# A planned TensorE order that counts the change between 64-row and 128-row matmuls and places like matmuls side by side, with 107 instead of 108 tiles on VectorE

## The chip, the cores and the metric

The kernel runs on one core of one Trainium2 chip. The metric is the device time of one execution in microseconds (us); lower is better. Times are medians of several executions. All the runs used here are undisturbed ("fast"). "Span" is the length of the one execution that was profiled; it is about 2 us shorter than the time that is measured around it.

## The reference, cut to what matters

```python
B, H, S, D = 1, 32, 2048, 640          # head size Dh = D // H = 20

def reference(q, k, v, t):
    eps = 1e-6
    qn = q / (jnp.sqrt((q * q).sum(axis=-1, keepdims=True)) + eps)
    kn = k / (jnp.sqrt((k * k).sum(axis=-1, keepdims=True)) + eps)
    logits = jnp.einsum('bhqd,bhkd->bhqk', qn, kn) * t[None, :, None, None]
    attn = _softmax(logits, axis=-1)
    return jnp.einsum('bhqk,bhkd->bhqd', attn, v)
```

It is attention with normalised q and k, for 32 heads of 2048 rows of 20 numbers. The expensive part is the exponential of 32 x 2048 x 2048 scores. The scores are cut into 512 row-tiles (16 per head), each 128 keys by 2048 queries.

## The kernel before

ScalarE computes the exponential of 404 of the 512 tiles, in 539 "waves" of up to three pieces of 128x512. VectorE computes the other 108 with integer and fp16 arithmetic. TensorE computes all scores (matmuls into `psA` for ScalarE, into `psD` for VectorE) and all sums with the values (matmuls into `psO`).

The three engines run fixed instruction lists. A small planner makes them when the kernel is built: each task has an engine, a duration, dependencies and a priority (lower goes first). The planner steps through time on a clock of its own, and whenever an engine is free it takes the ready task of the lowest priority. What the chip then does is bound to this order, but not to the planner's clock.

```python
    def schedule(self):
        ...                                            # cut
            for e in touched:
                if free[e] > now + 1e-9 or not ready[e]:
                    continue
                _, _, t = heapq.heappop(ready[e])      # lowest priority value
                t.start = now
                t.end = now + t.dur
                if e == "PE":
                    kind = t.name[:2]                  # "qk" or "pv"
                    if kind != last_pe[0]:
                        t.end += 0.09                  # a change of kind
                    last_pe[0] = kind
```

One wave's scores are two tasks. Heads have only 20 rows, zero-padded to 32, so the operands of two pieces from different halves of the array are multiplied at the same time with 64 rows each (the "pair"); the third piece is multiplied with 128 rows. Both tasks are named `qkA`:

```python
    pair = [] if plain else next(([i, i + 1] for i in range(len(us) - 1)
                if A_units[us[i]][2] // 2 != A_units[us[i + 1]][2] // 2), [])
    ...                                                # cut
    qks = [add("PE", f"qkA{w}", lambda e, tk, part=part: f_qk(e, part, 32 if plain else 64 if part is pair else 128),
               PE_MM * (1 if plain or part is pair else len(part)), deps, due_a(us[0]) - 100) for part in parts]
```

VectorE's scores are single 128-row matmuls, one for each 512 columns. They share one PSUM bank, so the next one can only be written when VectorE has read the last (`t1_prev`). Four such reads make a tile, and four more VectorE operations finish it:

```python
    for g in reversed(range(NG)):
        dep = [trn[h]] + rot[h] + (qz0 if h == 0 and j else []) + [t1_prev[0]]
        qk = add("PE", f"qkD{j}.{g}", lambda e, tk, h=h, r=r, g=g, j=j: qk_mm(
            e, h, r, g, psD[:, :], 128 if j else 32), PE_MM, dep, due - 50)
        ...                                            # cut: psD -> xt on VectorE
```

The sums with the values are groups of four matmuls that use 32 columns of the array each (`pvA`, `pve`, `pvs`, `pvt`, priority `due`).

## Time and profile before

| | before |
|---|---|
| time | 755.69 us (755.17 to 755.82, 3 executions); 755.43 us when timed beside the changed kernel |
| span of the profiled execution | 753.2 us |
| exponentials | 539, the shortest time from start to start 1.330 us |
| first exponential starts, last one starts | 14.05 us, 747.58 us |

The page of the profile of the kernel before: the span, the busy time of each engine with its share of the span and its number of instructions, and the shares of the chain of waits that ended last.

```profile
span 753.2 us, 12434 instructions
...
PE 702.4 (93%) x4960; PEld 194.6 (26%) x4960; DVE 719.6 (96%) x1209; ACT 731.7 (97%) x541; POOL 9.2 (1%) x24
...
ACT 59%; PE 23%; DVE 15%; DMA 1%; issue 1%; SPq 0%; DVEq 0%
```

Three engines are over 93% busy. The chain alternates among all of them: 59% ScalarE, 23% TensorE, 15% VectorE. So for 41% of the span it was not ScalarE itself that set the time.

The costliest groups (operation, shapes, count | busy us, mean ns of one | idle us before them and what ended it):

```profile
L489 ACT ACTIVATE p_ring<-psA 128x1536 bf16<-128x1536 f32 x539 | 730.2, 1523 | 15.7 <-PE psA L415 14.5
...
L522 DVE TENSOR_SCALAR xt<-psD 128x512 int16<-128x512 f32 x432 | 295.4, 684 | 23.1 <-PE psD L415 18.6
```

The mean of 1,523 ns is not the pace of ScalarE, because successive exponentials overlap in the record. Their start times are the better measure, and from them I made the following account. Each span splits exactly into four parts: the start of the first exponential; the number of intervals times the floor of 1.330 us; the loss, which is the sum of what each interval has above 1.330 us; and the tail from the start of the last exponential to the end. For before: 14.05 + 538 x 1.330 + 18.00 + 5.64 = 753.2 us. Of the loss, 3.34 us fall before 40 us, in the start, and 14.66 us after.

From the list of waits (engine, line, what it waited for: us in total, times, longest; "PEld" is TensorE's weight load, which comes first and so waits first):

```profile
PEld psA L415 <- ACT p_ring L489: 124.4, 356, 1.0
...
PEld psD L415 <- DVE xt L522: 63.1, 177, 1.3
DVE xt L522 <- PE psD L415: 18.6, 41, 1.2
...
ACT p_ring L489 <- PE psA L415: 14.5, 9, 11.4
```

The last line holds the 11.4 us at the start and little else: most of the misses are too small to show as idle time between overlapping records. The second line is TensorE waiting for VectorE to free the one PSUM bank.

TensorE's timeline near the end of before (start, duration, operation, rows*columns of the array, count):

```profile
739.17 0.40 PE L424 MATMUL psO<-p_ring,vaug 128*32 128x512 bf16 x4
739.50 0.39 PE L415 MATMUL psD<-qz,qkT 128*128 128x512 bf16 x1
739.82 0.39 PE L415 MATMUL psA<-qz,qkT 64*128 64x512 bf16 x2
740.14 0.39 PE L415 MATMUL psA<-qz,kR 128*128 128x512 bf16 x1
740.46 0.40 PE L424 MATMUL psO<-p_ring,vaug 128*32 128x512 bf16 x4
```

Every step changes the shape (32-column values, 128-row score, 64-row pair, 128-row score, values), and from start to start each takes 0.32 or 0.33 us. Over the whole trace, the step from a 128-row score in `psA` to one in `psD` takes 0.227 us in the median, and the step from a 64-row pair to the 128-row score 0.319 us. A change costs some 0.093 us.

### The profile page before, as it was taken

What the parts mean: (1) busy time and instruction counts of PE and PEld (TensorE: products, weight loads), DVE (VectorE), ACT (ScalarE), POOL (GpSimd) and SP (SyncE); (2) the same over time, 40 slices, a digit from 0 to 9 for tenths busy, and PEclk for the clock granted to TensorE, in tenths of its full rate; (3) what the DMA queues carried; (4) which work ended last, traced back from release to release, by engine and by line L of the source; (5) the groups of instructions that cost most, each with busy time, mean ns of one, the idle gap of its engine ahead of it and who ended that gap; (6) DMA issues with size and microseconds to landing.
All of it is one profiled execution on the core that took longest, in us unless ns stands there. A gap on an engine that the chain in (4) does not pass through costs nothing.

```text
span 753.2 us, 12434 instructions
## 1 busy us (share of the span) xinstructions
PE 702.4 (93%) x4960; PEld 194.6 (26%) x4960; DVE 719.6 (96%) x1209; ACT 731.7 (97%) x541; POOL 9.2 (1%) x24
## 2 busy tenths in 40 slices
PE   1999999999999999999999999999999999999997
PEld 0222222222222222222222222222222222222222
DVE  7799999999999999999999999999999999999997
ACT  3899999999999999999999999999999999999997
POOL 4000000000000000000000000000000000000000
PEclk9999999999999999999999999999999999999999
DMA  5533242323423242250323413234141332413000
GB/s 76 84 38 54 42 75 33 73 22 68 53 37 72 24 81 29 55 66 19 78 24 66 55 29 71 21 66 54 37 76 9 82 39 46 70 28 72 5 5 5
DMA packets 197929, 36.49 MB, mean 48 GB/s; under 512 B 173680, under 2 KB 197872, under 8 KB 197872
## 3 DMA queue, kind: packets, MB, share of 16 engines
q1 hardware_dynamic: 197728, 35.62, 29.6%
q8 instruction: 39, 0.64, 0.4%
q14 instruction: 18, 0.15, 0.1%
q10 hardware_dynamic: 144, 0.08, 0.1%
HBM read 7.87 MB, written 2.62 MB: 14 GB/s over the span
## 4 chain that ended last, share of the span: by engine, by line
ACT 59%; PE 23%; DVE 15%; DMA 1%; issue 1%; SPq 0%; DVEq 0%
ACT p_ring L489 59%; PE psA L415 11%; PE psO L424 8%; DVE xt L522 6%; PE psD L415 5%; DVE tt L536 4%; DVE mm L534 1%; DVE ee L530 1%; DVE ss L532 1%; DVE sq L320 1%; DVE rs_sum L322 1%; DMA kR<-kx 1%; SPq L234 0%; DVE qkn L348 0%; DMA qk_sb<-in_k_dram 0%
## 5 line engine op out<-in xcount | busy, mean ns | idle before, releaser
L489 ACT ACTIVATE p_ring<-psA 128x1536 bf16<-128x1536 f32 x539 | 730.2, 1523 | 15.7 <-PE psA L415 14.5
L415 PE MATMUL psA<-qz,kR 64*128 64x512 bf16 (+1 forms) x1209 | 319.0, 389 | 13.9 <-ACT p_ring L489 10.7
L522 DVE TENSOR_SCALAR xt<-psD 128x512 int16<-128x512 f32 x432 | 295.4, 684 | 23.1 <-PE psD L415 18.6
L424 PE MATMUL psO<-p_ring,vaug 128*32 128x512 bf16 x1616 | 152.1, 388 | 0.6 <-DVE oT L436 0.4
L415 PEld LDWEIGHTS psA<-qz,kR 64*128 64x128 bf16 (+1 forms) x1209 | 83.4, 94 | 225.3 <-issue 128.4
L415 PE MATMUL psA<-qz,qkT 64*128 64x512 bf16 (+1 forms) x392 | 128.6, 388 | 4.0 <-ACT p_ring L489 3.2
L536 DVE TENSOR_TENSOR tt<-xt,mm 128x2048 f16<-128x2048 f16 x108 | 131.0, 1213 | 0.2
L415 PE MATMUL psD<-qz,kR 128*128 128x512 bf16 x321 | 124.0, 386 | 6.0 <-DVE xt L522 3.8
L530 DVE TENSOR_SCALAR ee<-xt 128x2048 int16<-128x2048 int16 x108 | 73.7, 682 | 0.4
L534 DVE TENSOR_SCALAR mm<-xt 128x2048 int16<-128x2048 int16 x108 | 73.8, 684 | 0.0
L532 DVE TENSOR_SCALAR ss<-xt 128x2048 int16<-128x2048 int16 x108 | 73.7, 683 | 0.0
L424 PEld LDWEIGHTS psO<-p_ring,vaug 128*32 128x32 bf16 x1616 | 38.5, 94 | 84.6 <-issue 74.9
L415 PEld LDWEIGHTS psA<-qz,qkT 64*128 64x128 bf16 (+1 forms) x392 | 31.3, 94 | 68.9 <-issue 41.5
L415 PEld LDWEIGHTS psD<-qz,kR 128*128 128x128 bf16 x321 | 31.0, 97 | 65.8 <-DVE xt L522 43.6
L424 PE MATMUL psO<-tt,vaug 128*32 128x512 f16 x432 | 42.8, 386 | 3.4 <-DVE tt L536 2.0
L424 PE MATMUL psO<-ee,vaug 128*32 128x512 f16 x432 | 43.1, 389 | 1.5 <-DVE ee L530 1.3
L415 PE MATMUL psD<-qz,qkT 128*128 128x512 bf16 x107 | 41.5, 388 | 2.2 <-DVE xt L522 1.1
L424 PE MATMUL psO<-ss,vaug 128*32 128x512 f16 x432 | 42.7, 386 | 0.1
L320 DVE TENSOR_TENSOR sq<-qk_sb 128x640 f32<-128x640 bf16 x32 | 26.0, 813 | 0.9 <-DMA qk_sb<-in_q_dram 0.9
L322 DVE TENSOR_REDUCE rs_sum<-sq 128x32 f32<-128x640 f32 x32 | 25.7, 804 | 0.1
L348 DVE TENSOR_TENSOR qkn<-qk_sb,rs_r 128x640 bf16<-128x640 bf16 x31 | 25.2, 815 | 0.1
L436 DVE STREAM_TRANSPOSE oT<-psO 128x512 f32<-128x512 f32 x32 | 22.7, 709 | 2.1 <-PE psO L424 2.1
(36 smaller groups left out, 117.9 us busy)
## 6 DMA issues: line engine op xcount, KB each, us to landing
kR<-qkT SPq DMA_DIRECT2D x62, 96.0 KB, 2.1
qz<-qkT SPq DMA_DIRECT2D x128, 32.0 KB, 1.9
kR<-qkT SPq DMA_DIRECT2D x62, 64.0 KB, 2.0
qk_sb<-in_k_dram SPq DMA_DIRECT2D x32, 80.0 KB, 2.1
vaug<-in_v_dram SPq DMA_DIRECT2D x32, 80.0 KB, 3.3
qk_sb<-in_q_dram SPq DMA_DIRECT2D x124, 20.0 KB, 2.5
out_dram<-o_stage SPq DMA_DIRECT2D x31, 80.0 KB, 1.9
kR<-qkT SPq DMA_DIRECT2D x62, 32.0 KB, 1.9
```

Source lines behind the costliest of these rows:

```text
L320: s1 = dv("sq", lambda e, tk, x=x: e.tensor_tensor(sq[:, :, :], x[:, :, :], x[:, :, :], ALU.mult), 0.86, lds[h] + last_sum)
L322: sums.append(dv("sum", lambda e, tk, i=i: e.tensor_reduce(rs["sum"][:, 2 * R * i:2 * R * (i + 1)], sq[:, :, :], AXIS_X, ALU.add), 0.86, [ ...
L348: norm[h] = dv("norm", lambda e, tk, x=x, b=b, i=i: e.tensor_tensor(qkn[b][:, :, 0:D], x[:, :, :], bc(rs["r"][:, 2 * R * i:2 * R * (i + 1) ...
L415: return eng.matmul(dst, lhsT, mov, tile_position=(p0, 0))
L424: last = eng.matmul(psO[32 * g:32 * g + 32, :], vaug[h % NV][:, r_of(g), :], rhs_of(g), start=start, stop=False, skip_group_check=True, ti ...
L436: trO[h] = add("DVE", f"tr{h}", lambda e, tk: e.transpose(oT[:, :, :].rearrange("p r d -> p (r d)"), psO[:, :]), 0.63, [lambda: pv_users[h ...
L489: act[w] = add("ACT", f"exp{w}", lambda e, tk: e.activation(p_ring[:, p0 * 512:p0 * 512 + n], psA[:, slot * WAVE * 512:slot * WAVE * 512 + ...
L522: t1_prev[0] = add("DVE", f"t1.{j}.{g}", lambda e, tk, o=o: e.tensor_scalar(xt[sx][:, o:o + 512], psD[:, :], X_MUL, X_ADD, ALU.mult, ALU.a ...
L530: te = dv("e", lambda e, tk: e.tensor_scalar(ee[se][:, 0:w], x, 0x7C00, KE_BITS, ALU.bitwise_and, ALU.bitwise_or), 0.533, t1s + old("e", NE))
L532: t5 = dv("s", lambda e, tk: e.tensor_scalar(ss[se][:, 0:w], x, float(SHIFT - 4096), None, ALU.add), 0.533, t1s + old("s", NE))
L534: tm = dv("m", lambda e, tk: e.tensor_scalar(mm[sm][:, 0:w], x, 0x3FF, 0x3800, ALU.bitwise_and, ALU.bitwise_or), 0.533, t1s + old("m", NM))
L536: tT = dv("T", lambda e, tk: e.tensor_tensor(tt[se][:, 0:w], x.bitcast(FP16), mm[sm][:, 0:w].bitcast(FP16), ALU.mult), 1.067, [tm] + old(" ...
```

## The change: its intent, and the diff

The intent is that the planner counts what the chip charges. The 64-row pair gets a name of its own (`q2`), so that the change between 64 and 128 rows costs 0.09 us in the plan as well. TensorE then prefers a ready task of the kind that ran last: the others are treated as if they were due 0.3 heads later. VectorE's scores lose their absolute priority (`due - 50` becomes `due - 0.5`), so that this preference can act on them. One tile moves from VectorE to ScalarE, and the lead with which heads are prepared shrinks from 2.4 to 2.1 heads.

```diff
--- before.py
+++ after.py
@@ -43,8 +43,11 @@
 
     SEM_LAT = {"PE": 0.18, "ACT": 0.15, "DVE": 0.10, "POOL": 0.15, "SP": 0.0}
 
+    SWITCH = 0.3
+
     def __init__(self):
         self.tasks = []
+        self.nsw = 0
 
     def add(self, eng, name, fn, dur, deps=(), pri=0.0, lat=0.0, dma=None):
         t = Task(eng, name, fn, dur, deps, pri, lat, dma)
@@ -91,13 +94,20 @@
             for e in touched:
                 if free[e] > now + 1e-9 or not ready[e]:
                     continue
-                _, _, t = heapq.heappop(ready[e])
+                if e == "PE":
+                    x = min(ready[e], key=lambda r: (r[0] + (0.0 if r[2].name[:2] == last_pe[0] else self.SWITCH), r[1]))
+                    ready[e].remove(x)
+                    heapq.heapify(ready[e])
+                    t = x[2]
+                else:
+                    _, _, t = heapq.heappop(ready[e])
                 t.start = now
                 t.end = now + t.dur
                 if e == "PE":
                     kind = t.name[:2]
                     if kind != last_pe[0]:
                         t.end += 0.09
+                        self.nsw += 1
                     last_pe[0] = kind
                 free[e] = t.end
                 order[e].append(t)
@@ -194,9 +204,9 @@
     WPLAIN = 5
     EARLY = 3
     NSOLO = 4
-    LEAD = 2.4
+    LEAD = 2.1
     PE_MM = 0.23
-    DVE_TILES = [4 if h % 3 == 1 or h == 14 else 3 for h in range(H)]
+    DVE_TILES = [4 if h % 3 == 1 else 3 for h in range(H)]
 
     with ExitStack() as es:
         sbuf = lambda name, shape, dt: es.enter_context(nc.sbuf_tensor(name, shape, dt))
@@ -479,7 +489,7 @@
             for h in hs:
                 moved = any(A_units[u][0] == h and (A_units[u][1] - A_units[u][2]) % 4 for u in us)
                 deps += [trn[h]] + (rot[h] if h or moved else rot[h][:1]) + ([] if h or plain else qz0)
-            qks = [add("PE", f"qkA{w}", lambda e, tk, part=part: f_qk(e, part, 32 if plain else 64 if part is pair else 128),
+            qks = [add("PE", f"q{'2' if part is pair else 'k'}A{w}", lambda e, tk, part=part: f_qk(e, part, 32 if plain else 64 if part is pair else 128),
                        PE_MM * (1 if plain or part is pair else len(part)), deps, due_a(us[0]) - 100) for part in parts]
             for h in hs:
                 qk_users[h] += qks
@@ -516,7 +526,7 @@
                 for g in reversed(range(NG)):
                     dep = [trn[h]] + rot[h] + (qz0 if h == 0 and j else []) + [t1_prev[0]]
                     qk = add("PE", f"qkD{j}.{g}", lambda e, tk, h=h, r=r, g=g, j=j: qk_mm(
-                        e, h, r, g, psD[:, :], 128 if j else 32), PE_MM, dep, due - 50)
+                        e, h, r, g, psD[:, :], 128 if j else 32), PE_MM, dep, due - 0.5)
                     qk_users[h].append(qk)
                     o = 2048 * i + 512 * g
                     t1_prev[0] = add("DVE", f"t1.{j}.{g}", lambda e, tk, o=o: e.tensor_scalar(
```

## The prediction

> **What bounds the kernel now.** ScalarE. The page of the profile gives it 731.7 us busy of a 753.2 us span; VectorE has 719.6, TensorE 702.4. Start-to-start times of the 539 exponentials, read from the timeline, show a floor of 1.330 us (351 of 538 intervals). The first starts at 14.05 us, the last at 747.58, the program ends at 753.2. So 538 x 1.330 = 715.5 us is floor and 18.0 us is lost between exponentials: 3.3 us before 40 us, and 14.6 us spread evenly over the rest, as misses of 0.02 to 0.3 us: ScalarE waits there for TensorE's scores, late in its planned order.
>
> **TensorE.** In the timeline, one score matmul or one group of four value matmuls takes 0.226 us from start to start when the next has the same shape (128-row score to 128-row score), and 0.319 us when it differs (64-row to 128-row score, or score to 32-column value): a change costs 0.093 us. The Trainium skill, "TensorEngine Tiling (Array Packing)", Key Properties, says that changing the tiling mode drains TensorE; this trace agrees. From the instruction order I count 2,232 such slots and about 1,792 changes before. Estimate: 2,232 x 0.226 + 1,792 x 0.093 = 671 us of some 735: per exponential 1.24 of 1.33 us. The old planner saw 969 changes, since 64-row and 128-row scores had one name.
>
> **What the change does.**
> 1. The planner sees the 64/128 change and prefers the like kind. By the new order the changes fall to 1,555: 237 x 0.093 = 22 us less TensorE work (estimate 649 us). VectorE's score matmuls now stand next to the 128-row ones of the exponentials. It is not on the critical path itself: it buys TensorE slack, about 0.09 to 0.13 us per exponential.
> 2. VectorE has 107 tiles instead of 108: minus 4 x 0.684 + 3 x 0.683 + 1.213 = 6.0 us on VectorE, plus four 512-column pieces, one more exponential, plus about 1.3 us on ScalarE, the bottleneck.
> 3. VectorE's score matmuls lose their absolute priority over value matmuls. That can starve VectorE, which has one PSUM bank and no second buffer. The shorter lead of the preparation (2.4 to 2.1 heads) should do nothing.
>
> **On the critical path.** Plus 1.3 us for the extra exponential; minus a part of the 14.6 us. I expect about half of those, 7 us, to go: misses caused by TensorE's total load shrink with the slack, while those from its fixed order (a matmul at the head waiting for VectorE) stay. Net about -5.5 us.
>
> **Predicted time: 750.0 us**, 0.7% less; 8 in 10: 745.5 to 755.5. Removing every lost microsecond outside the start would give about 742, still under 2% less, so faster by over 2%: 0.02; within 2%: 0.96; slower by over 2%: 0.02.
>
> **What would show it.** Right: 540 exponentials at the same 1.330 us floor; loss between them after 40 us down from 14.6 to about 7; TensorE's waits for the exponentials longer in the list of waits; VectorE about 714 us busy with more idle time. Wrong: VectorE's waits for its scores clearly above 18.6 us, and ScalarE's loss unchanged.
>
> **What would make it wrong.** The lost time may be set by order and latencies rather than by load: then nothing is regained and it ends near 757. VectorE starved by the lower priority would make its tiles late and block TensorE's in-order queue: slower.

## The result, and the profile after

| | before | after |
|---|---|---|
| time, median of 4 | 755.43 us (754.94 to 755.82) | 749.6 us (748.85 to 750.18) |
| ratio of fast runs | | 0.9923, 95% interval 0.9905 to 0.994 |
| span | 753.2 us | 746.8 us |

A ratio is the mean time of one kernel's fast runs over that of the other's fast runs of the same rounds, so it is not quite the ratio of the medians in the table.

The page of the changed kernel, the same lines (line numbers moved by 10):

```profile
span 746.8 us, 12310 instructions
...
PE 672.8 (90%) x4862; PEld 191.9 (26%) x4952; DVE 714.2 (96%) x1201; ACT 727.8 (97%) x542; POOL 9.2 (1%) x24
...
ACT 93%; DVE 2%; DMA 2%; PE 1%; SPq 1%; issue 0%; ACTq 0%
```

The chain of waits now runs through ScalarE for 93% of the span instead of 59%. This is the clearest single reading of what happened: the other two engines almost never set the time any more. ScalarE's share of busy time is 97% in both pages and could not have told it.

```profile
L499 ACT ACTIVATE p_ring<-psA 128x1536 bf16<-128x1536 f32 x540 | 726.3, 1668 | 13.7 <-PE psA L425 13.7
...
L532 DVE TENSOR_SCALAR xt<-psD 128x512 int16<-128x512 f32 x428 | 293.0, 685 | 20.3 <-PE psD L425 13.9
```

ScalarE has one exponential more (540). VectorE has 428 reads of scores instead of 432. Its idle time before them, 20.3 us, is a little less than the 23.1 us of before.

```profile
PEld psA L425 <- ACT p_ring L499: 157.6, 410, 0.9
...
PEld psD L425 <- DVE xt L532: 50.8, 151, 1.3
...
DVE xt L532 <- PE psD L425: 13.9, 29, 1.2
...
ACT p_ring L499 <- PE psA L425: 13.7, 5, 11.9
```

TensorE waits longer for ScalarE to free the scores' banks (157.6 us instead of 124.4): its weights stand ready earlier, so the scores come in time. VectorE waits less for its scores, not more (13.9 instead of 18.6 us).

```profile
730.48 0.40 PE L434 MATMUL psO<-tt,vaug 128*32 128x512 f16 x4
730.81 0.39 PE L425 MATMUL psA<-qz,kR 64*128 64x512 bf16 x1
730.82 0.39 PE L425 MATMUL psA<-qz,qkT 64*128 64x512 bf16 x1
731.13 0.39 PE L425 MATMUL psA<-qz,kR 128*128 128x512 bf16 x1
731.36 0.38 PE L425 MATMUL psD<-qz,kR 128*128 128x512 bf16 x1
731.67 0.40 PE L434 MATMUL psO<-p_ring,vaug 128*32 128x512 bf16 x4
```

Here a 128-row score for ScalarE (731.13) and one for VectorE (731.36) stand side by side, and the step between them takes 0.23 us. The steps that still change take 0.31 to 0.33 us, as before.

The account of the start times says where the 6.4 us of span went:

| | exponentials | first starts | floor | loss before 40 us | loss after 40 us | tail | span |
|---|---|---|---|---|---|---|---|
| before | 539 | 14.05 | 715.5 | 3.34 | 14.66 | 5.64 | 753.2 |
| after | 540 | 14.60 | 716.9 | 2.21 | 7.33 | 5.84 | 746.8 |
| difference | +1 | +0.55 | +1.3 | -1.1 | -7.3 | +0.2 | -6.4 |

The gain is the halved loss after 40 us, less the extra exponential. Intervals that are more than 0.05 us too long fell from 98 to 32.

### The profile page after: what moved, and what is told of

Same layout as the page of the kernel before. It is cut to its first block, busy times and chain, and to the rows that moved or that the text cites. A ratio compares the mean times of both kernels' runs of the same rounds, so it can differ in the third digit from the quotient of the medians.

```text
span 746.8 us, 12310 instructions
## 1 busy us (share of the span) xinstructions
PE 672.8 (90%) x4862; PEld 191.9 (26%) x4952; DVE 714.2 (96%) x1201; ACT 727.8 (97%) x542; POOL 9.2 (1%) x24
## 4 chain that ended last, share of the span: by engine, by line
ACT 93%; DVE 2%; DMA 2%; PE 1%; SPq 1%; issue 0%; ACTq 0%
ACT p_ring L499 93%; SPq L244 1%; PE psA L425 1%; DMA kR<-kx 1%; DMA qk_sb<-in_q_dram 1%; DVE sq L330 0%; PE psD L425 0%; DVE xt L532 0%; PE psO L434 0%; DMA qkT<-qkn 0%; DMA qk_sb<-in_k_dram 0%; DVE rs_sum L332 0%; ACTq L211 0%; DVE tt L546 0%; DVE rs_u L335 0%
## 5 line engine op out<-in xcount | busy, mean ns | idle before, releaser
L425 PE MATMUL psA<-qz,kR 64*128 64x512 bf16 (+1 forms) x1170 | 305.0, 388 | 26.2 <-ACT p_ring L499 18.9
L532 DVE TENSOR_SCALAR xt<-psD 128x512 int16<-128x512 f32 x428 | 293.0, 685 | 20.3 <-PE psD L425 13.9
L425 PE MATMUL psA<-qz,qkT 64*128 64x512 bf16 (+1 forms) x382 | 124.1, 387 | 6.8 <-ACT p_ring L499 4.4
L425 PE MATMUL psD<-qz,kR 128*128 128x512 bf16 x292 | 112.4, 385 | 9.3 <-DVE xt L532 4.6
L425 PEld LDWEIGHTS psD<-qz,kR 128*128 128x128 bf16 x318 | 30.7, 97 | 55.4 <-DVE xt L532 34.5
L425 PE MATMUL psD<-qz,qkT 128*128 128x512 bf16 x95 | 36.6, 385 | 3.3 <-issue 1.1
```

Source lines behind the costliest of these rows:

```text
L425: return eng.matmul(dst, lhsT, mov, tile_position=(p0, 0))
L532: t1_prev[0] = add("DVE", f"t1.{j}.{g}", lambda e, tk, o=o: e.tensor_scalar(xt[sx][:, o:o + 512], psD[:, :], X_MUL, X_ADD, ALU.mult, ALU.a ...
```

## The experiments

Twelve kernels ran, all with correct results, each timed in 5 rounds against the kernel before. One table holds all the accounts, all from one profiled execution each, in us. "Of it, half clock" is the loss in intervals that lie wholly in (or end within 1.5 us behind) a window in which the throttle granted TensorE half its clock. "Stalls" is the sum of single losses of 1 us or more after 40 us, and "other loss" is the rest of the loss after 40 us. "VectorE's end" is the time from the start of the last exponential to the end of VectorE's last tile.

| run | ratio to before | loss after 40 us | of it, half clock | stalls | other loss | VectorE's end | tail |
|---|---|---|---|---|---|---|---|
| before | 1 | 14.66 | 0 | 0 | 14.66 | 1.29 | 5.64 |
| after | 0.9923 | 7.33 | 0 | 0 | 7.33 | 1.25 | 5.84 |
| after_again | 0.9913 | 8.05 | 0 | 0 | 8.05 | 1.25 | 5.85 |
| b_107 | 0.9979 | 13.85 | 0 | 0 | 13.85 | -5.34 | 5.85 |
| a_108 | 1.0072 | 11.04 | 0 | 3.48 | 7.56 | 11.75 | 16.10 |
| b_64 | 1.0030 | 11.95 | 5.87 | 4.15 | 7.80 | 1.18 | 5.53 |
| a_extra | 0.9935 | 10.21 | 0 | 0 | 10.21 | 1.05 | 5.63 |
| b_64a | 0.9899 | 7.86 | 0 | 0 | 7.86 | 1.33 | 5.67 |
| b_names | 1.0159 | 15.32 | 0 | 7.58 | 7.74 | 12.26 | 16.61 |
| a_prio50 | 1.0009 | 8.55 | 0 | 1.06 | 7.48 | 7.17 | 11.52 |
| a_noswitch | 1.0057 | 12.36 | 1.84 | 3.95 | 8.41 | 8.07 | 12.42 |
| a_extra2 | 1.0056 | 17.36 | 0 | 0 | 17.36 | 1.23 | 5.67 |
| a_lead24 | 0.9974 | 10.11 | 0.81 | 1.49 | 8.63 | 4.57 | 8.70 |
| a_mix | 0.9914 | 6.81 | 0 | 0 | 6.81 | 1.26 | 5.85 |

The first theory (A) is that of the prediction: fewer changes mean less TensorE work, the slack lets the scores come in time. Rivals: the 6.0 us taken off VectorE are the gain (B); the order, planned with true costs, is the gain and not the load (C); later also that VectorE's lower priority lets the exponentials' scores through (D), and that VectorE's position in the plan decides (E).

### b_107: one tile fewer, nothing else

```diff
-    DVE_TILES = [4 if h % 3 == 1 or h == 14 else 3 for h in range(H)]
+    DVE_TILES = [4 if h % 3 == 1 else 3 for h in range(H)]
```

> The kernel before with nothing changed but 107 VectorE tiles instead of 108; the planner stays as it was (about 1,812 changes of TensorE mode in the order). Theory A (the gain is TensorE load taken off by fewer changes): no gain from this part, ScalarE has one exponential more, ratio to before 1.000 to 1.003 (755 to 758 us), loss between exponentials after 40 us still 12 to 16 us. Rival B (VectorE, 96% busy, was the real limit and the 6.0 us taken off it are the gain): ratio 0.991 to 0.994 (about 750 us), VectorE busy near 714 us.

Measured: 755.79 us, ratio 0.9979 (0.9957 to 1.0001), loss after 40 us 13.85. That is just below A's range of ratios, and A's range of loss holds. In these rounds the kernel before itself fell into two groups, three executions at 755.5 us and eight at 758.8 us in the mean; in all other rounds it shows the first group alone. Five of the six executions of b_107 lie in the lower group too, and against the three of before they give 1.0005, which is inside A's range. The ratios of a_108, b_64 and a_extra come from the same rounds and carry the same blur, up to 0.003. B as the whole cause is out. VectorE's last tile was ready 5.34 us before the last exponential began; in the old order that spare time bought next to nothing.

### a_108: the changed kernel with 108 tiles

```diff
-    DVE_TILES = [4 if h % 3 == 1 else 3 for h in range(H)]
+    DVE_TILES = [4 if h % 3 == 1 or h == 14 else 3 for h in range(H)]
```

> The changed kernel with 108 VectorE tiles again (539 exponentials; about 1,525 changes in the order, as few as in the changed kernel). Theory A: the gain stays, and one exponential less makes it as fast or 1.3 us faster than the changed kernel, ratio to before 0.989 to 0.993. Rival B (VectorE's 6 us are the gain): the gain goes, ratio 0.998 to 1.002.

Measured: 763.64 us, ratio 1.0072 (1.0048 to 1.0097). Both theories missed; it is slower than before. The last exponentials of this run, then VectorE after them:

```profile
738.95 9.37 ACT L499 ACTIVATE p_ring<-psA 128x1536 bf16<-128x1536 f32 x7
```

```profile
753.72 1.21 DVE L546 TENSOR_TENSOR tt<-xt,mm 128x2048 f16<-128x2048 f16 x1
...
757.50 1.23 DVE L546 TENSOR_TENSOR tt<-xt,mm 128x2048 f16<-128x2048 f16 x1
759.45 0.72 DVE L446 STREAM_TRANSPOSE oT<-psO 128x512 f32<-128x512 f32 x1 [0.72 <-PE psO L434]
```

ScalarE's last record ends at 738.95 + 9.37 = 748.32 us, about where it ends in before, but VectorE's last two tiles are only finished at 754.9 and 758.7, and the output waits for them. The tail is 16.1 us instead of 5.8. ScalarE's small misses stayed at the low level (7.56 us), so the order's benefit is there and is buried under VectorE's lateness. (This profile and that of b_64 also began some 3 us later, because the first scores' operand landed at 16.8 and 16.7 instead of 13.4 us. Before that, VectorE's first operation, a conversion of `t`, had taken 5.87 and 5.88 us instead of 0.29; neither edit touches it. This may be what parts the two groups of times in these rounds, 3 us from each other, but before was not profiled in them.)

### b_64: the old order with less TensorE work

```diff
-        ... f_qk(e, part, 32 if plain else 64 if part is pair else 128),
+        ... f_qk(e, part, 32 if plain else 64),
-        e, h, r, g, psD[:, :], 128 if j else 32), PE_MM, dep, due - 50)
+        e, h, r, g, psD[:, :], 64 if j else 32), PE_MM, dep, due - 50)
```

> The kernel before in exactly its own order, but every score matmul after the first waves is a 64-row one, so that only changes between scores and values are left: about 970 instead of 1,792, 822 x 0.093 = 76 us less TensorE work, and no new plan. Theory A (load): loss between exponentials after 40 us falls from 14.6 us to 2 to 6 us, ratio 0.984 to 0.990. Rival C (the new plan, not the load, made the gain): loss stays at 11 us or more, ratio 0.996 to 1.002.

Measured: 760.32 us, ratio 1.003 (0.9997 to 1.0064). Its time, just above C's range, and its whole loss of 11.95 us spoke for C; its profile does not. Here are some windows of 3.4 us of that run (busy us and number of instructions of each engine, then the granted clock):

```profile
core 0: us, PE busy (x) PEld busy (x) DVE busy (x) ACT busy (x) POOL busy (x), PEclk, DMA share, GB/s
209.00:212.40 3.40, 1.91 (x19) 0.43 (x11) 3.40 (x6) 3.40 (x4) 0.00 (x0) 1.00 0.05 2
212.40:215.80 3.40, 3.40 (x21) 0.56 (x19) 2.48 (x4) 3.40 (x3) 0.00 (x0) 0.50 0.00 0
570.80:574.20 3.40, 2.26 (x15) 0.54 (x15) 3.40 (x5) 3.40 (x4) 0.00 (x0) 1.00 0.52 30
642.50:645.90 3.40, 2.34 (x15) 0.59 (x15) 3.40 (x6) 3.40 (x4) 0.00 (x0) 1.00 0.38 95
```

The second window was granted half the clock (0.50), and the window before it had TensorE busy for only 1.91 of 3.40 us. Two more such windows, at 574.2 and from 645.9 us on, follow stretches of 2.26 and 2.34 us busy. The start also stayed at half clock until 45.1 us (26.1 in before). The Trainium skill, "TensorE: Matmul & The Clock Gate", Part 1, describes a gate that watches activity in windows of 3413 ns and grants either half or all of the clock; the clock record here agrees, with windows of 3.41 us and the two values 0.5 and 1. So with this lighter load TensorE ran ahead, waited for ScalarE (the longest waits in these three stretches are 0.74, 0.66 and 0.52 us) and was throttled. Whether the shorter busy time alone lowered the clock, or also that 64-row matmuls use half of the rows, is not separated by this run. Of the loss of 11.95 us, 5.87 lie at half clock; what is left, 6.08 us, is under half of before's 14.66.

### a_extra and a_extra2: the changed order with work given back

```diff
                     last = qk_mm(eng, h, r, g, psA[:, ...], rows)
+                    if rows == 128 and w % 11 in (5, 10):        # a_extra: 98 waves
+                        last = qk_mm(eng, h, r, g, psA[:, ...], rows)
```

The second kernel has `(2, 5, 8, 10)`, 195 waves.

> The changed kernel in exactly its own order with the 22 us of TensorE work given back: in two of every eleven waves (98 waves) the 128-row score matmul of the exponentials is done twice into the same place (same result, 98 x 0.226 = 22 us, no further change of mode). Theory A (load): loss between exponentials after 40 us rises from 7.3 us to 11 to 16 us, ratio to before 0.997 to 1.003. Rival C (plan): loss rises by less than 2 us, ratio 0.992 to 0.995.

> The changed kernel in its own order with twice the extra TensorE work: 195 waves do their 128-row score matmul twice, 195 x 0.226 = 44 us; load is then 22 us above that of before. Theory A (load alone sets the loss): loss after 40 us 15 us or more, above that of before; ratio 1.000 to 1.010. Mixed theory (load and an order planned with true costs both count; the run with 22 us extra had 10.2 us): loss 11 to 15 us, below that of before although the load is higher, ratio 0.995 to 1.001.

Measured: a_extra 752.93 us, ratio 0.9935 (0.9913 to 0.9957), loss after 40 us 10.21; a_extra2 760.01 us, ratio 1.0056 (1.0044 to 1.0069), loss 17.36. With the 22 us the loss fell between the ranges of A and C. The ratio lies in C's range, but the two groups of times blur it: the five lower executions against the three lower ones of before give 0.996, between the ranges too. The 44 us fell in A's, above those of the mixed theory. So load does count: with the order fixed, the loss goes from 7.3 and 8.1 (two profiles) to 10.2 and 17.4. But with the 22 us given back the loss is still 4.4 us below that of before. The extra work does not stand where the changes stood, so this is not a proof that the order is worth just that much.

### b_64a: the old order with a smaller dose taken away

```diff
-        ... f_qk(e, part, 32 if plain else 64 if part is pair else 128),
+        ... f_qk(e, part, 32 if plain else 64 if part is pair or w >= 40 else 128),
```

> The kernel before in its own order and with its own planner; from wave 40 on the exponentials' single score matmul is a 64-row one too, while VectorE's scores stay 128-row. About 1,467 changes instead of 1,792: 325 x 0.093 = 30 us less TensorE work, a dose near the 22 us of the change, and more of the array stays in use than when all scores had 64 rows. Theory A (load): loss between exponentials after 40 us falls from 14.7 to 5 to 8 us, none of it at half clock; ratio 0.988 to 0.993. Rival C (the plan made the gain): loss at 11 us or more, ratio 0.996 to 1.002. Theory F (less TensorE activity makes the clock fall to half for windows of 3.4 us, as in the run with 64 rows everywhere): such windows appear here too and take the gain back.

Measured: 748.32 us, ratio 0.9899 (0.9883 to 0.9914), loss after 40 us 7.86, none at half clock. A's ranges hold, C's and F's do not. The order and the plan are those of before, VectorE keeps its 108 tiles, and the gain is at least as large as that of the whole change. One of its waves on the timeline:

```profile
731.11 0.39 PE L415 MATMUL psA<-qz,kR 64*128 64x512 bf16 x1 [0.26 <-issue]
731.12 0.39 PE L415 MATMUL psA<-qz,qkT 64*128 64x512 bf16 x1
731.34 0.38 PE L415 MATMUL psA<-qz,kR 64*128 64x512 bf16 x1
731.65 0.40 PE L424 MATMUL psO<-p_ring,vaug 128*32 128x512 bf16 x4
```

The single score follows its 64-row pair after 0.22 us instead of 0.32.

### b_names: only the true cost in the plan

```diff
-            qks = [add("PE", f"qkA{w}", ...
+            qks = [add("PE", f"q{'2' if part is pair else 'k'}A{w}", ...
```

> The kernel before with one thing changed: 64-row and 128-row scores have different names, so the planner charges 0.09 us for the change between them, but chooses as before, by priority alone, with 108 tiles. 1,749 changes in the order, so only 4 us less TensorE work. Theory A (load): loss after 40 us stays at 12 to 15 us. Rival C (a plan with true costs is what counts): loss below 9 us. Theory E (with true costs the plan puts VectorE's tiles late; in the planner's own clock this plan ends 17 us later than that of before, as the one with 108 tiles in the changed kernel did by 11): the tail after the last exponential grows from 5.6 to 15 us or more, ratio 1.008 to 1.020.

Measured: 767.73 us, ratio 1.0159 (1.0145 to 1.0173), the slowest of all. The loss of 15.32 us is outside both ranges, just above A's, and it is made of other things than before: three stalls (2.84, 3.25 and 1.49 us) hold 7.58 us, and the small misses that made up the 14.66 us are down to 7.74. The removed work is only 43 changes, 4 us. So a plan with true costs cuts the small misses nearly without cutting load: C is right in this, though not in its number. VectorE's work being put off past the end does not explain it: between the 20th and the 150th exponential the small misses are already 1.85 us, against 3.68 in before, and at the 135th VectorE is only one tile behind (25 instead of 26). VectorE's last tile comes 12.26 us after the last exponential, and the tail of 16.61 us is what E expected.

### a_prio50: VectorE's scores at the old priority

```diff
-  ... psD[:, :], 128 if j else 32), PE_MM, dep, due - 0.5)
+  ... psD[:, :], 128 if j else 32), PE_MM, dep, due - 50)
```

> The changed kernel with VectorE's score matmuls at their old, absolute priority (due - 50 instead of due - 0.5); 1,526 changes, even fewer. Theory A (load): loss after 40 us 6 to 9 us, ratio 0.990 to 0.994. Rival D (the lower priority of VectorE's scores lets the exponentials' chain through and is the gain): loss 11 us or more, ratio 0.997 to 1.001. Theory E (the planner's own clock ends 6.5 us later than the changed kernel's): VectorE's last tile is late and the tail grows by some 6 us, ratio 0.998 to 1.003 with a small loss.

Measured: 755.87 us, ratio 1.0009 (0.9996 to 1.0022): the whole gain is gone, although the changes are fewer still. The loss, 8.55 us, is as low as A said. The time went into the tail (11.52 us), because VectorE's end is 7.17 us behind the last exponential. E holds; D's range of ratios holds too, but not its loss. In this plan the absolute priority of VectorE's scores made VectorE later, not earlier.

### a_noswitch: without the preference for the like kind

```diff
-    SWITCH = 0.3
+    SWITCH = 0.0
```

> The changed kernel without the preference for the like kind (penalty 0 instead of 0.3), the rest as changed: 1,745 changes, 190 x 0.093 = 18 us more TensorE work than the changed kernel. Theory A (load): loss after 40 us 11 to 14 us, ratio 0.997 to 1.001. Rival C (true costs in the plan, not the load): loss 8 us or less. Theory E (planner's own clock ends 7 us later): tail grows by some 7 us.

Measured: 759.77 us, ratio 1.0057 (1.0044 to 1.007), above A's range. The loss of 12.36 us is in A's range, but 3.95 us of it are two stalls. With 18 us more TensorE work the small misses are 8.41 us, hardly above the 7.3 and 8.1 of the changed kernel: the fewer changes as such bought little there. What the preference bought is elsewhere. The tail is 12.42 us, and two stalls led to windows at half clock. TensorE's timeline shows how the first one began:

```profile
110.10 0.71 PE L425 MATMUL psA<-qz,kR 64*128 64x512 bf16 x3
112.83 0.39 PE L425 MATMUL psD<-qz,qkT 128*128 128x512 bf16 x1 [2.02 <-DVE xt L532]
```

The score matmul for VectorE stood at the head of TensorE's queue and waited 2.02 us for VectorE to read the bank. Nothing behind it ran in that time. The windows around it:

```profile
core 0: us, PE busy (x) PEld busy (x) DVE busy (x) ACT busy (x) POOL busy (x), PEclk, DMA share, GB/s
107.30:110.70 3.40, 3.40 (x34) 0.92 (x30) 1.61 (x2) 3.40 (x3) 0.00 (x0) 1.00 0.71 45
110.70:114.10 3.40, 1.16 (x8) 0.39 (x8) 2.75 (x5) 1.84 (x2) 0.00 (x0) 0.99 0.43 63
114.10:117.50 3.40, 3.34 (x15) 0.73 (x15) 3.04 (x5) 2.90 (x2) 0.00 (x0) 0.51 0.63 37
```

TensorE was busy for 1.16 of 3.40 us, and in the next window its clock was 0.51 in the mean. The loss in half-clock windows is 1.84 us, a part of the 8.41.

### a_lead24: the preparation's lead

```diff
-    LEAD = 2.1
+    LEAD = 2.4
```

> The changed kernel with the preparation's lead at 2.4 heads again; 1,548 changes. If the lead does nothing, as predicted: ratio 0.990 to 0.994, loss after 40 us 6 to 9 us, tail under 6 us. Theory E (the planner's own clock ends this plan 3 us later because VectorE's tiles come late): tail longer by 2 to 4 us, ratio 0.995 to 0.999.

Measured: 753.87 us, ratio 0.9974 (0.9962 to 0.9987), tail 8.70 us, loss 10.11 of which 0.81 at half clock. The lead is worth about 0.6% (0.9974 against the 0.9913 of the changed kernel on the same chip), by way of VectorE's end (4.57 instead of 1.25 us) and of some loss. E's ranges hold.

### a_mix and after_again

```diff
+        pe = [x.name for x in prog.order["PE"]]
+        for a, b, c in zip(pe, pe[1:], pe[2:]):
+            if b[:3] == "qkA" and int(b[3:]) >= 40 and a[:3] != "qkD" and c[:3] != "qkD":
+                lone.add(b)
...
-        ... 32 if plain else 64 if part is pair else 128),
+        ... 32 if plain else 64 if part is pair or f'qkA{w}' in lone else 128),
```

> The changed kernel in its own order; from wave 40 on an exponentials' single score matmul that does not stand next to one of VectorE's is a 64-row one: 95 changes fewer (about 1,464), 9 us less TensorE work. Theory A and the mixed theory: loss after 40 us falls by 1 to 3 us to 4.5 to 6.5 us, ratio 0.988 to 0.991, unless VectorE's end or a window at half clock takes it back.

> The changed kernel again, unedited, for its spread and to stand beside the three others of this chip. Ratio to before 0.990 to 0.994; in its profile loss after 40 us 6 to 9 us, tail 5.5 to 6.0 us, VectorE's last tile ready about 1.3 us after the last exponential starts.

The unedited changed kernel measured 749.44 us, ratio 0.9913 (0.99 to 0.9927), loss 8.05: it repeats. With 9 us less TensorE work in its order, a_mix measured 749.22 us, ratio 0.9914 (0.99 to 0.9927), loss 6.81. The expected further gain is not there in the time, and the loss of 6.81 us is above the expected range. At this level, more slack for TensorE is worth nothing that these runs can show. The best median is that of b_64a, 748.32 us; its interval, 0.9883 to 0.9914, overlaps that of the changed kernel, and the two were never timed on the same chip in the same rounds, so I don't call one faster.

## Why the prediction was right or wrong, point by point

- **The time and the account.** Predicted 750.0 us, measured 749.6. The sum was predicted as +1.3 us for one exponential and -7 us from the loss; measured +1.3 and -7.3, with -0.4 us from start and tail together. Part of this is luck: "about half" of the loss was a guess, and nothing in the prediction gives 7 us rather than 3 or 11. The sum also needed parts that the forecast gave no worth: with any one of four of them taken away the kernel ends at 753.87 to 763.64 us. To take ScalarE as the bound, and its pace from start times and not from busy shares, was right: the chain of waits went from 59% to 93% ScalarE.
- **A change costs 0.093 us and 1,555 are left.** Right: these steps have the same medians, 0.319 and 0.227 us, in both traces. The records of before hold 1,792 changes; those of after hold 1,540, with 90 of the 4,952 matmuls missing from the trace, against 1,555 in the order as built. The Trainium skill, "TensorEngine Tiling (Array Packing)", Key Properties, names the drain, and these steps agree with it.
- **"misses caused by TensorE's total load shrink with the slack".** Right but not the whole cause. That load moves the loss was shown twice: 30 us taken off the old order brought it from 14.66 to 7.86 us, and 44 us put on the new order brought it from 7.33 (or 8.05) to 17.36. But b_names and a_noswitch have nearly the TensorE work of before, and their small misses are 7.74 and 8.41 us. Planning with the true cost is enough for that by itself, though these plans bring stalls and a late VectorE with them. The two ways do not add up; both end near 7 us. How much of the change's 7.3 us to assign to each stays open. The prediction had the fact in hand (the old planner saw 969 changes of 1,792) and gave it no part in the sum.
- **What the preference does.** I credited the 237 removed changes with the gain. Without the preference (a_noswitch) the small misses stay low; what comes back is VectorE's lateness (tail 12.42 us), stalls and half-clock windows. Its worth lies there.
- **"VectorE has 107 tiles".** The 1.3 us on ScalarE were right. What I did not say is that the tile is a condition of the gain: with 108 tiles the changed kernel takes 763.64 us, because VectorE ends 11.75 us after the last exponential starts. Already in before VectorE ended 1.29 us after that start. It had no time to spare, and I had read only ScalarE as the bound.
- **"VectorE's score matmuls lose their absolute priority ... That can starve VectorE".** The sign was wrong. VectorE's waits for scores fell from 18.6 to 13.9 us, and restoring the priority made VectorE 7.17 us late and cost the whole gain.
- **"The shorter lead ... should do nothing".** Wrong: it is worth about 0.6%, some two thirds of the whole change. The prediction gave no reason. The lead is also the priority by which preparation competes with VectorE's tiles in the plan, and VectorE's end moved.
- **"VectorE about 714 us busy with more idle time".** The first half is right (714.2), the second is not: up to the end of its last tile VectorE is idle for 30.7 us before and 29.5 us after.

So the forecast was right in its sum, and its mechanism was shown to be able to give that sum. But four of the change's five parts (the preference, the priority, the tile and the lead) were shown to work, wholly or in part, by something that the forecast did not have: they bring VectorE home together with ScalarE. The lateness is made in the plan and not on the chip. Building the kernels again, without running them, gives the planner's own clock, in which VectorE's last tile ends this long after the start of the last exponential:

| us | before | after | a_lead24 | a_prio50 | a_noswitch | a_108 | b_names |
|---|---|---|---|---|---|---|---|
| planned | 0.84 | 0.93 | 4.36 | 7.06 | 7.78 | 11.31 | 11.82 |
| measured | 1.29 | 1.25 | 4.57 | 7.17 | 8.07 | 11.75 | 12.26 |

The two stalls of a_108 and the two largest of b_names stand in the plan as well, before the same exponentials. The small misses do not: in the plan of before no exponential after 40 us is late. Why the planner, once it charges the true cost, puts VectorE's tiles late is not settled by these runs.

## What to carry to other kernels

When a planner fixes the order of an engine's work, give it the costs that the chip charges, and then look at when every engine finishes its last piece, since the same correction can move another engine past the end. Here the planner's own clock showed this before anything ran. Measure the pace of a saturated engine from start to start and sum the excess; busy shares hid a loss of 18 us here and hid its halving too. Before crediting one part of a compound change, take each part away alone: here each of the four parts that were removed alone cost from two thirds of the gain to more than all of it.

## What the Trainium skill lacked or had wrong

- "TensorE: Matmul & The Clock Gate" (table of advice: no idle gaps over about 3 us between matmul bursts): not enough here. In a_noswitch a single gap of 2.02 us in TensorE's work, in a window with 1.16 of 3.40 us busy, was followed by a window at half clock; in b_64 windows with 1.91, 2.26 and 2.34 us busy were, with no gap above 0.74 us. In its part on a second failure mode the page does tell of short idle times that make the clock swing, but it does not say how much activity in a window keeps the clock up. A fixed threshold of busy time can't be read from these runs either, since in b_64a a stretch with 2.21 of 3.40 us busy (from 116.1 us on) kept the full clock.
- "TensorEngine Tiling (Array Packing)", Key Properties: it says that a change of mode drains TensorE, but not what this costs. Here it was 0.093 us for each of 64 to 128 rows and 128-column scores to 32-column values (0.319 against 0.226 us from start to start).
- The same page recommends small tiles for small operands and is silent on the clock: with 64-row scores everywhere, TensorE's start at half clock lasted until 45.1 us instead of 26.1 (a_108, whose start was late by the same 3 us, had the full clock from 29.6 us on).
